# A new order of work inside the groups of a fused retention and feed-forward kernel

## The chip, the cores and the metric

The kernel runs on one core of a Trainium2 chip. A core has TensorE (PE in the profile; its weight loads are PEld), VectorE (DVE), ScalarE (ACT), GpSimd (POOL) and SyncE (SP, which here issues transfers). The time is device time in microseconds of one execution; a time of a version is the median of several runs. A profile is one execution recorded instruction by instruction.

## The reference

Two layers, one behind the other. The first is retention, linear attention with a decay for each of 8 heads; the second is a feed-forward pair of matrices with a leaky ReLU.

```python
def _attn_ref(q, k, v):                # 8 x 8 heads x 576 x 64
    scores = scale * np.matmul(q, k.transpose(0, 1, 3, 2))
    gamma = 1.0 - 2.0 ** (-5.0 - np.arange(H))
    Dmat = np.where(rel >= 0, gamma[:, None, None] ** rel[None], 0.0)   # rel = i - j
    return np.matmul(scores * Dmat[None], v)

def _moe_ref(x, w_in, w_out):          # x: 4608 tokens x 512, d_ff 2048
    h = x @ w_in
    g = np.maximum(0.01 * h, h)
    return g @ w_out
```

## The kernel before

The 4608 tokens are cut into 9 groups of 512 (`g` = 0 to 8) and 36 units of 128 (`u`, four to a group). A unit of retention is loaded (q, k, v), cast to 16 bits with its decay (`kc` on ScalarE, `qc` and `vc` on GpSimd), transposed by a transfer, and multiplied: scores and the state of two chunks of 64, then the outputs. While TensorE does the feed-forward part of group g, it does the retention of units that belong to the next group.

Retention of one unit, as steps of a group (`n` = 5 to 8, `u` = 4g + n):

```python
def mm():                        # "sc": scores of u, then outputs of the unit before
    if u < NU:
        scores(u)                # lines L225, L234; PSUM tile sc, one buffer
    outputs(u - 1)               # lines L316 (masked scores), L327 (state); PSUM tile ot
ops = {"sc": mm, "own": lambda: own(u - 1), "add": lambda: add(u - 1)}
ops["s0"] = lambda: state(u, 0)              # VectorE, L278 to L286
ops["s1a"] = lambda: state(u, 1, (0,))
ops["s1"] = lambda: state(u, 1, (1,))
ops["stc"] = lambda: state_cast(u, pool_copy)      # GpSimd, L298 and L301
if n < 7:
    ops["mc"] = lambda: masks_aside(u, 0)          # ScalarE copies the scores, L244
    ops["msk"] = lambda: masks_aside(u, 1)         # GpSimd masks them, L246
else:
    ops["msk"] = lambda: masks(u)                  # VectorE masks them, L255
# w = u + 2: the unit whose casts run in this step
ops["kc"] ... cast_k(w)   ops["qc"] ... cast_q(w, nc.gpsimd)   ops["vc"] ... cast_v(w, nc.gpsimd)
# when k and q are cast: transpose_dma(w), then load(u + 4)
```

The first product of the feed-forward part has 16 blocks of 128 columns of `w_in`. Four blocks at a time (a set: A = 0, 1, 8, 9; B = 2, 3, 10, 11; C = 4, 5, 12, 13) are done with seven products in place of eight, in the manner of Strassen and Winograd; this needs sums of the weights (`w_sum`, made once: `sum_w_in(f, n, engine)`, f = 0, 2, 4 for A, B, C), sums of x for each group (`x0` to `x3` on GpSimd, `sum_x`, L469), and sums of the products on VectorE. Blocks 6, 7, 14, 15 are done plainly, with four matmuls of 512 columns (L401).

```python
ops = {   # one set; a product is four matmuls of 256 columns, L498
    "p1": product("p1", ws(0, 0), xs(0, 0), True),   "k": keep(),               # ScalarE copy
    "p1'": product("p1", ws(0, 1), xs(1, 0), False), "g00": give(0, 0, "p1"),   # ScalarE, leaky
    "p6": product("p6", w(1), t(1), True),           "u": into(k, p6, k),       # VectorE, L487
    "p5": product("p5", w(0), t(0), True),           "v": fresh_sum("v", p5, k),
    "p7": product("p7", w(2), t(2), True),           "h4": into(v, p7, v),
    "p5'": product("p5", w(3), xs(1, 1), False),     "h5": fresh_sum("h", p5, k),
    "g11": give(1, 1, "v"),
    "p7'": product("p7", ws(1, 1), t(3), False),     "h4'": into(k, p7, k),
    "g01": give(0, 1, "h"),                          "g10": give(1, 0, "k"),
}
```

The second product (`w_out`) is done as one such set over the whole group: seven products of 16 matmuls of 256 columns (L636). Its sums of g are the mix sums of VectorE, in halves: `m00`, `m01`, `m10`, ... `m31` (L618, both inputs in SBUF). `m3` is written over a part of `gt` that P1 has read, and is an input of P5'; `m2` likewise for P7; P5 needs `m0`, P6 needs `m1`. `K` and `o00` are ScalarE copies, `U`, `V`, `o11`, `o01`, `o10` VectorE sums.

The order in which each engine gets its work is the order of this text; engines run their own queues in order and wait for each other only where data or buffers ask for it:

```python
GROUP = """
    p1A kA sc5 p6A qc5 s05 kc5 s1a5 p1'A mc5 p5A uA s15 blk15 own5 vA vc5 g00A add5 p7A
    msk5 stc5 l15 p1B h4A p5'A h5A kB sc6 kc6 p7'A p1'B p6B mc6 own6 s06 h4'A g00B blk7
    ...
    vc6 s17 qc7 l6 vc7 h4C stc7 kc7 h5C g11C add7 P1 g01C g10B m00 p7'C sc8 m01 own8 P5
    h4'C qc8 m10 m11 P6 K g10C m20 vc8 add8 m21 P7 kc8 U s08 V s1a8 m30 P1' x0 x1 m31 P5'
    s18 o11 x2 stc8 o00 msk8 P7' o01 o10 x3
"""
```

PSUM[...]: the tiles `sc` and `ot` take two each, and the four banks called `acc` go round among all products and blocks. The casts have four buffers, the loads five.

Groups 0 and 1 have an order of their own. Around the second product of groups 0 and 1:

```python
def burst(u, out=True):     # scores(u), outputs(u-1), VectorE's mask and state, GpSimd's state_cast
def ahead(u, between=None): # cast_k, cast_q (GpSimd), between(), cast_v (GpSimd), transpose
at = {
    ...
    12: lambda: [sum_w_in(0, n, nc.vector) for n in range(4)]
    + [nc.vector.tensor_copy(out=mask16, in_=mask_sb)],
    9: lambda: early(9, 12),                      # burst(9), ahead(12), load(15)
    13: lambda: [sum_w_in(2, n, nc.gpsimd) for n in range(4)],
}
... # second product of group 0 in 16 parts, with at[n] behind part n
burst(10)
ops = second_ops(1, {})
run("P1 K m30 m31")
early(11, 13)                                     # burst(11), ahead(13), load(16)
for n in range(4):
    sum_w_in(4, n, nc.gpsimd)
run("P1' o00 P6 U P5 V")
burst(12)
sum_x(2, (0, 1))
ahead(14, lambda: sum_x(2, (2, 3)))
load(17)
run("P7 o11 P5' o01 P7' o10")
```

Groups 2 to 7 follow `GROUP`, group 8 follows a list `LAST` without retention.

Of the kernel before, what the change touches and what calls it, by code (L numbers as in the profile page):

```python
# [18 lines left out]
def kernel(  # L19
# [9 lines left out]
    nc = tc.nc  # L29
    B, H, S, D = q.shape  # L30
# [53 lines left out]
    def behind(dma, *others):  # L84
        for o in others:
            tc.add_manual_dep(
                dma.ins,
                o.ins.name,
                mybir.DependencyInfo(
                    mybir.DependencyClass.Sync, mybir.DependencyReason.DATA  # L90
                ),
                reason="order of loads",
            )
# [6 lines left out]
    mask_sb = cs[:, NTAB : NTAB + CH]  # L100
# [9 lines left out]
    mask16 = idle[:, 0:CH]  # L110
# [10 lines left out]
    def load(u, eng=None, after=None, xs=(1, 0, 2)):  # L121
        for x in xs:
            t = ld_pool.tile([P, H, D], FP, name=f"t32_{x}")
            t32[u, x] = t
            c = 2 * u
            same = c % CB + 1 < CB
            e = eng[x] if isinstance(eng, dict) else eng or nc.sync
            engs = e if isinstance(e, tuple) else (e,)
            n = H // len(engs)
            for j, rows in ((0, P),) if same else ((0, CH), (1, CH)):  # L130
                b, w = (c + j) // CB, (c + j) % CB
                for i, e in enumerate(engs):
                    hs = slice(n * i, n * i + n)
                    d = e.dma_start(
                        out=t[CH * j : CH * j + rows, hs],
                        in_=(q, k, v)[x][b, hs, CH * w : CH * w + rows, :].rearrange(
                            "h t d -> t h d"
                        ),
                    )
                    if after is not None and (x in after or not isinstance(after, dict)):  # L140
                        behind(d, *(after[x] if isinstance(after, dict) else after))
                        after = None
                    last_load[u, x] = d
# [33 lines left out]
    def cast_k(u):  # L177
        nc.scalar.copy(out=qk_of(u)[:, 1], in_=t32[u, 1])

    def cast_q(u, eng):  # L180
        eng.tensor_tensor(out=qk_of(u)[:, 0], in0=t32[u, 0], in1=decay(u, 0), op=MUL)  # L181
# [71 lines left out]
    def masks(u):  # L253
        s16s[u] = b_pool.tile([P, 2, NP, CH], F16, name="s16")
        nc.vector.tensor_tensor(  # L255
            out=s16s[u],
            in0=sc_tiles[u][:, :, 0],
            in1=mask_sb.unsqueeze(1).unsqueeze(1).to_broadcast([P, 2, NP, CH]),
            op=MUL,
        )  # L260
# [34 lines left out]
    def state_cast(u, copy, js=(0, 1)):  # L295
        js = [j for j in js if live(u, j)]
        if len(js) == 2:
            copy(out=st16[u], in_=s32s[u])  # L298
        else:
            for j in js:  # L300
                copy(out=st16[u][:, j], in_=s32s[u][:, j])  # L301
# [79 lines left out]
    def own(u):  # L381
        owns[u] = b_pool.tile([P, NP, 2, CH], FP, name="own")
        nc.scalar.copy(  # L383
            out=owns[u], in_=ot_tiles[u][:, :, 0:NP].rearrange("q j c t -> q c j t")
        )
# [13 lines left out]
    def h_mm(hps, n, g, f, ts):  # L399
        for c in range(NP):  # L400
            nc.tensor.matmul(  # L401
                out=hps[:, n, :],
                lhsT=w_in16[:, c, f * P : (f + 1) * P],
                rhs=xT[g][:, c, ts],
                start=(c == 0),
                stop=(c == NP - 1),
            )

    def g_tile(g):
        if g not in g_t:  # L410
            g_t[g] = g_pool.tile([P, NF, TOK], F16, name="gt")
        return g_t[g]

    def leaky(out, in_):
        nc.scalar.activation(out=out, in_=in_, func=mybir.ActivationFunctionType.Lrelu)  # L415
# [23 lines left out]
    def w_sub(f, i, j):  # L439
        c0 = (f + i * HF) * P  # L440
        return w_in16[:, 2 * j : 2 * j + 2, c0 : c0 + 2 * P]

    def x_sub(g, j, k):
        return xT[g][:, 2 * j : 2 * j + 2, k * HT : (k + 1) * HT]

    def sum_w_in(f, n, eng):
        t = w_sum[:, f // 2]
        a, b, op = (
            (w_sub(f, 1, 0), w_sub(f, 1, 1), ADD),
            (t[:, 0], w_sub(f, 0, 0), SUB),  # L450
            (w_sub(f, 0, 0), w_sub(f, 1, 0), SUB),
            (w_sub(f, 0, 1), t[:, 1], SUB),
        )[n]
        eng.tensor_tensor(out=t[:, n], in0=a, in1=b, op=op)  # L454
# [3 lines left out]
    def sum_x(g, ns=range(4)):  # L458
        if g not in x_sums:
            x_sums[g] = s_pool.tile([P, 4, NP // 2, HT], F16, name="x_sum")  # L460
        t = x_sums[g]
        for n in ns:
            a, b = (
                (x_sub(g, 0, 1), x_sub(g, 0, 0)),
                (x_sub(g, 1, 1), t[:, 0]),
                (x_sub(g, 1, 1), x_sub(g, 0, 1)),
                (x_sub(g, 1, 0), t[:, 1]),
            )[n]
            nc.gpsimd.tensor_tensor(out=t[:, n], in0=a, in1=b, op=SUB)  # L469
# [10 lines left out]
    def bank(home, shape=(P, 2, HT)):  # L480
        pool, name = {
            None: (acc_pool, "acc"), "sc": (sc_pool, "sc"), "ot": (ot_pool, "ot")
        }[home]
        return pool.tile(list(shape), FP, name=name)
# [66 lines left out]
    def block_ops(g, f, homes):  # L551
        t = {}

        def mm():
            t["h"] = bank(homes.get(f"Bk{f}"), (P, 1, TOK))
            h_mm(t["h"], 0, g, f, slice(0, TOK))

        return {f"blk{f}": mm, f"l{f}": lambda: leaky(g_tile(g)[:, f : f + 1, :], t["h"])}
# [278 lines left out]
    def burst(u, out=True):  # L837

        scores(u)
        if out:  # L840
            outputs(u - 1)
        masks(u)
        state(u, 0)
        state(u, 1)
        state_cast(u, pool_copy)
        if out:
            own(u - 1)
            add(u - 1)

    def ahead(u, between=None):  # L850

        if u < NU:
            cast_k(u)
            cast_q(u, nc.gpsimd)
        if between is not None:
            between()
        if u < NU:
            cast_v(u, nc.gpsimd)
            transpose_dma(u)

    def step_ops(g, n):
# [39 lines left out]


    GROUP = """
        p1A kA sc5 p6A qc5 s05 kc5 s1a5 p1'A mc5 p5A uA s15 blk15 own5 vA vc5 g00A add5 p7A
        msk5 stc5 l15 p1B h4A p5'A h5A kB sc6 kc6 p7'A p1'B p6B mc6 own6 s06 h4'A g00B blk7
        msk6 s1a6 qc6 p5B uB p1C s16 vB g01A l7 p6C add6 g10A p7B kC h4B g11A p5'B stc6 p1'C
        g00C sc7 p7'B h5B uC s07 blk14 own7 msk7 p5C blk6 h4'B vC s1a7 p7C g11B p5'C g01B l14
        vc6 s17 qc7 l6 vc7 h4C stc7 kc7 h5C g11C add7 P1 g01C g10B m00 p7'C sc8 m01 own8 P5
        h4'C qc8 m10 m11 P6 K g10C m20 vc8 add8 m21 P7 kc8 U s08 V s1a8 m30 P1' x0 x1 m31 P5'
        s18 o11 x2 stc8 o00 msk8 P7' o01 o10 x3  # L910
    """
    LAST = """
        p1A blk6 p6A kA l6 uA p5A vA p7A p1'A p6B g00A p1B p5'A h4A kB h5A p6C p7'A uB p1'B
# [89 lines left out]
    def early(u, n):  # L1003
        burst(u)
        ahead(n)
        load(n + 3)
# [4 lines left out]
        3: lambda: mixes(1, 1),  # L1011
        4: lambda: (burst(8, False), ahead(11), load(13), load(14)),
        7: lambda: mixes(1, 2),
        12: lambda: [sum_w_in(0, n, nc.vector) for n in range(4)]
        + [nc.vector.tensor_copy(out=mask16, in_=mask_sb)],
        9: lambda: early(9, 12),
        13: lambda: [sum_w_in(2, n, nc.gpsimd) for n in range(4)],
    }
    for n in range(16):
        if n:  # L1020
            wide(n // 4, n % 4)
        if n in at:
            at[n]()
    burst(10)
    ops = second_ops(1, {})
    run = lambda names: [ops[n]() for n in names.split()]
    run("P1 K m30 m31")
    early(11, 13)
    for n in range(4):
        sum_w_in(4, n, nc.gpsimd)  # L1030
    run("P1' o00 P6 U P5 V")
    burst(12)
    sum_x(2, (0, 1))
    ahead(14, lambda: sum_x(2, (2, 3)))
    load(17)
    run("P7 o11 P5' o01 P7' o10")

    for g in range(2, NG):
        last = g == NG - 1
        homes = LAST_HOMES if last else {}  # L1040
        ops = second_ops(g, homes, last)
        for s, f in SETS.items():
            ops.update(set_ops(g, f, s, homes))
        for f in BLOCKS:
            ops.update(block_ops(g, f, homes))
        if not last:
            for n in range(5, 9):
                ops.update(step_ops(g, n))
            for n in range(4):
                ops[f"x{n}"] = lambda n=n: sum_x(g + 1, (n,))  # L1050
        for name in (LAST if last else GROUP).split():
            if name in ops:
                ops[name]()

# [29 lines left out]
```

## Time and profile before

| | |
|---|---|
| time, median of 3 runs | 292.82 us (292.59 to 293.51) |
| span of the profiled run | 292.1 us |
| mean granted clock of TensorE | 0.984 |
| HBM read, written | 36.81 MB, 9.44 MB |

The page of the profile starts with the busy time of each engine and its share of the span, then cuts the span into 40 equal slices of 7.3 us, in which each digit is a busy share in tenths:

```profile
PE   7899999997995999999999999999999999999993
DVE  2973888999763699889988997999799989977962
ACT  4767777432333671598059706870786078405900
POOL 8968847468799435774667466737573861160000
```

A busy TensorE is not a TensorE at its peak: the records overlap, and their ends are modelled. For its pace the starts of consecutive records are compared. The timeline lists instructions in order with the idle time before each and the engine whose signal ended it. "L618" is a line of the kernel; where a helper writes many tiles, all have its line, so the names of output and inputs tell them apart. The groups show in the slices as a period of about four digits from the 12th on.

### The profile page before, as it was taken

How to read it: one execution, taken by the hardware profiler on the slowest of the kernel's cores; microseconds unless marked ns; L12 is line 12 of the kernel's file. 1: busy time of each engine (PE TensorE's matmuls, PEld its weight loads, DVE VectorE, ACT ScalarE, POOL GpSimd, SP SyncE). 2: the span in 40 equal slices, each digit the busy share in tenths (PEclk: the TensorE clock that was granted, in tenths of full speed). 3: DMA queues.
4: the chain of work that ended last, by engine and by line, in shares of the span. 5: the costliest groups of instructions: out<-in, count | busy, mean ns of one | idle time of the engine just before them, and what ended most of it. 6: DMA issues, size and time to landing. Idle time of an engine off the chain costs nothing.

```text
span 292.1 us, 10069 instructions
## 1 busy us (share of the span) xinstructions
PE 276.1 (95%) x4317; PEld 214.3 (73%) x4317; DVE 240.5 (82%) x391; ACT 158.1 (54%) x291; POOL 170.1 (58%) x181
## 2 busy tenths in 40 slices
PE   7899999997995999999999999999999999999993
PEld 2578888545884677778777778788878787888782
DVE  2973888999763699889988997999799989977962
ACT  4767777432333671598059706870786078405900
POOL 8968847468799435774667466737573861160000
PEclk9999999999997799999999999999999999999998
DMA  8999999978999939888977788968988350002012
GB/s 223 292 223 219 289 209 328 209 162 198 251 215 274 186 73 217 165 191 181 189 211 175 172 173 191 200 143 195 201 196 182 42 183 3 0 36 109 2 38 108
DMA packets 123101, 50.05 MB, mean 171 GB/s; under 512 B 112048, under 2 KB 116784, under 8 KB 123056
## 3 DMA queue, kind: packets, MB, share of 16 engines
q1 hardware_dynamic: 116032, 37.23, 57.6%
q0 software_dynamic: 6736, 12.06, 17.2%
q8 instruction: 34, 0.56, 0.8%
q10 hardware_dynamic: 288, 0.11, 0.1%
q14 instruction: 11, 0.09, 0.1%
HBM read 36.81 MB, written 9.44 MB: 158 GB/s over the span
## 4 chain that ended last, share of the span: by engine, by line
PE 51%; DVE 33%; issue 6%; POOL 5%; ACT 2%; DMA 1%; DVEq 0%; POOLq 0%
PE acc L498 18%; PE acc L401 13%; PE acc L636 9%; DVE gt L618 7%; DVE mix L618 6%; DVE w_mix L599 4%; DVE k L487 3%; DVE xT L388 3%; DVE v L487 3%; PE sc L225 2%; POOL x_sum L469 2%; POOL w_sum L454 2%; DVE w_sum L454 2%; DVE h L487 1%; PE acc L708 1%
## 5 line engine op out<-in xcount | busy, mean ns | idle before, releaser
L636 PEld LDWEIGHTS <-gt 128*128 128x128 f16 x640 | 61.7, 98 | 11.7 <-DVE gt L618 4.1
L401 PE MATMUL acc<-xT,w_in 128*128 128x256 f16 (+2 forms) x376 | 58.6, 300 | 0.3 <-issue 0.3
L415 ACT ACTIVATE gt<-acc 128x512 f16<-128x512 f32 x77 | 45.8, 599 | 19.8 <-PE acc L401 14.6
L636 PE MATMUL acc<-w_out,gt 128*128 128x256 f16 x384 | 45.8, 273 | 2.4 <-DVE gt L618 2.3
L401 PEld LDWEIGHTS <-w_in 128*128 128x128 f16 x384 | 35.5, 98 | 11.4 <-issue 1.3
L498 PEld LDWEIGHTS <-w_sum 128*128 128x128 f16 x336 | 32.9, 99 | 10.7 <-issue 1.1
L487 DVE TENSOR_TENSOR k<-acc,k 128x512 f32<-128x512 f32 x48 | 32.6, 684 | 8.1 <-PE acc L498 6.1
L498 PE MATMUL acc<-x_sum,w_sum 128*128 128x256 f16 x244 | 36.3, 278 | 0.0
L469 POOL TENSOR_TENSOR x_sum<-xT 128x512 f16<-128x512 f16 x14 | 20.8, 1484 | 26.1 <-DVE xT L388 26.1
L185 POOL TENSOR_TENSOR v<-t,cs 128x512 f16<-128x512 f32 x28 | 30.8, 1101 | 0.5 <-DMA t<-in_v_dram 0.5
L181 POOL TENSOR_TENSOR qk<-t,cs 128x512 f16<-128x512 f32 x28 | 29.8, 1064 | 1.8 <-DMA t<-in_q_dram 1.7
L636 PE MATMUL acc<-w_mix,mix 128*128 128x256 f16 x256 | 29.8, 273 | 0.4 <-DVE mix L618 0.2
L636 PE MATMUL acc<-w_mix,gt 128*128 128x256 f16 x240 | 28.8, 272 | 0.0
L383 ACT COPY own<-ot 128x512 f32<-128x512 f32 x33 | 19.5, 590 | 16.6 <-PE ot L327 15.8
L521 ACT COPY k<-acc 128x512 f32<-128x512 f32 x19 | 11.1, 586 | 30.7 <-PE acc L498 30.5
L636 PEld LDWEIGHTS <-mix 128*128 128x128 f16 x256 | 24.1, 98 | 4.5 <-DVE mix L618 1.4
L498 PEld LDWEIGHTS <-w_in 128*128 128x128 f16 x252 | 24.1, 100 | 3.9 <-issue 0.2
L298 POOL CAST st<-s 128x512 f16<-128x512 f32 x21 | 12.8, 610 | 22.1 <-DVE s L284 18.2
L388 DVE TENSOR_TENSOR xT<-ot,own 128x512 f16<-128x512 f32 x33 | 22.5, 682 | 3.4 <-ACT own L383 3.4
L661 ACT COPY osb<-acc 128x512 f32<-128x512 f32 x8 | 4.7, 586 | 37.0 <-PE acc L636 37.0
L498 PE MATMUL acc<-xT,w_in 128*128 128x256 f16 x152 | 23.4, 277 | 0.0
L487 DVE TENSOR_TENSOR v<-acc,k 128x512 f32<-128x512 f32 x29 | 19.9, 686 | 4.1 <-PE acc L498 2.0
(95 smaller groups left out, 515.5 us busy)
## 6 DMA issues: line engine op xcount, KB each, us to landing
out_dram<-osb SPq DMA_DIRECT2D x17, 512.0 KB, 3.1
t<-in_k_dram SPq DMA_DIRECT2D x24, 256.0 KB, 3.7
t<-in_q_dram SPq DMA_DIRECT2D x23, 256.0 KB, 4.3
t<-in_v_dram SPq DMA_DIRECT2D x22, 256.0 KB, 4.4
t<-in_v_dram POOLq DMA_DIRECT2D x10, 256.0 KB, 5.9
t<-in_q_dram POOLq DMA_DIRECT2D x9, 256.0 KB, 5.6
t<-in_k_dram POOLq DMA_DIRECT2D x8, 256.0 KB, 7.5
w_in<-in_moe_w_in_dram POOLq DMA_DIRECT2D x8, 256.0 KB, 6.7
```

What stands on the lines that cost most here:

```text
L181: eng.tensor_tensor(out=qk_of(u)[:, 0], in0=t32[u, 0], in1=decay(u, 0), op=MUL)
L185: eng.tensor_tensor(out=v16[u], in0=t32[u, 2], in1=decay(u, 1), op=MUL)
L298: copy(out=st16[u], in_=s32s[u])
L383: nc.scalar.copy(out=owns[u], in_=ot_tiles[u][:, :, 0:NP].rearrange("q j c t -> q c j t"))
L388: nc.vector.tensor_tensor(out=x_of(u).rearrange("q (c g) t -> q c g t", g=2), in0=ot_tiles[u][:, :, NP : 2 * NP].rearrange("q g (c j) t -> ...
L401: nc.tensor.matmul(out=hps[:, n, :], lhsT=w_in16[:, c, f * P : (f + 1) * P], rhs=xT[g][:, c, ts], start=(c == 0), stop=(c == NP - 1),)
L415: nc.scalar.activation(out=out, in_=in_, func=mybir.ActivationFunctionType.Lrelu)
L469: nc.gpsimd.tensor_tensor(out=t[:, n], in0=a, in1=b, op=SUB)
L487: nc.vector.tensor_tensor(out=out, in0=a, in1=b, op=ADD)
L498: nc.tensor.matmul(out=r[name][:, n, :], lhsT=lhs()[:, c, n * P : (n + 1) * P], rhs=rhs()[:, c, :], start=fresh and n == 0 and c == 0, sto ...
L618: nc.vector.tensor_tensor(out=z[:, fs], in0=a[:, fs], in1=b[:, fs], op=op)
L636: nc.tensor.matmul(out=r[name][tb][:, 0, :] if apart else r[name][0][:, tb, :], lhsT=lhs()[:, f, tb * P : (tb + 1) * P], rhs=rhs[:, f, :], ...
```

## The change

Six edits:

1. The mask of 16 bits is cast by ScalarE and not by VectorE, and ahead of VectorE's weight sums.
2. The weight sums of set B (GpSimd) move from behind part 13 of group 0's second product to two places: two behind `burst(10)`, two behind the casts of units 13 and 14.
3. Unit 14 is cast with unit 13, ahead of P1', and no longer between the x sums of group 2. The loads of units 16 and 17 follow it.
4. Group 2 (the third) does set C as four plain blocks (4, 5, 12, 13), at the places of p1C, p6C, p5C and p7C.
5. So set C's weight sums are needed one group later; they move into group 2, still on GpSimd.
6. `GROUP` is a new order. Products and their sums stand closer to each other, unit 5 to 8's steps stand later, unit 8's scores stand behind P1', the mix sums are spread, `vc6`, `vc7`, `vc8`, `qc8` and the x sums stand later.

The aim is to keep VectorE's sums of two SBUF inputs and GpSimd's work apart in time, and to have unit 14 and GpSimd's masks ready sooner.

```diff
     GROUP = """
-        p1A kA sc5 p6A qc5 s05 kc5 s1a5 p1'A mc5 p5A uA s15 blk15 own5 vA vc5 g00A add5 p7A
-        msk5 stc5 l15 p1B h4A p5'A h5A kB sc6 kc6 p7'A p1'B p6B mc6 own6 s06 h4'A g00B blk7
-        msk6 s1a6 qc6 p5B uB p1C s16 vB g01A l7 p6C add6 g10A p7B kC h4B g11A p5'B stc6 p1'C
-        g00C sc7 p7'B h5B uC s07 blk14 own7 msk7 p5C blk6 h4'B vC s1a7 p7C g11B p5'C g01B l14
-        vc6 s17 qc7 l6 vc7 h4C stc7 kc7 h5C g11C add7 P1 g01C g10B m00 p7'C sc8 m01 own8 P5
-        h4'C qc8 m10 m11 P6 K g10C m20 vc8 add8 m21 P7 kc8 U s08 V s1a8 m30 P1' x0 x1 m31 P5'
-        s18 o11 x2 stc8 o00 msk8 P7' o01 o10 x3
+        p1A blk15 p6A kA p1'A g00A l15 p5A sc5 uA p7A kc5 vA p1B p5'A p6B s05 h4A own5 s1a5 kB
+        h5A p7'A s15 mc5 qc5 h4'A p1'B g00B g01A uB blk7 msk5 stc5 vc5 p5B l7 add5 p1C p7B sc6
+        g10A kC vB h4B g11A kc6 p5'B p1'C p7'B s06 h5B s1a6 p6C qc6 mc6 p5C msk6 g00C own6 g11B
+        h4'B uC blk6 p7C blk14 s16 vC vc6 add6 stc6 g01B g10B l6 p5'C l14 h4C sc7 g11C h5C p7'C
+        m00 qc7 g01C s07 h4'C m01 m10 P1 s1a7 m11 kc7 P5 own7 m20 K s17 P6 g10C m30 P1' msk7
+        stc7 add7 sc8 U m21 V m31 own8 P7 vc7 s08 add8 P5' o11 o00 x0 o01 kc8 P7' s1a8 qc8 x1
+        s18 x2 stc8 o10 x3 msk8 vc8
     """
...
-        12: lambda: [sum_w_in(0, n, nc.vector) for n in range(4)]
-        + [nc.vector.tensor_copy(out=mask16, in_=mask_sb)],
+        12: lambda: [nc.scalar.copy(out=mask16, in_=mask_sb)]
+        + [sum_w_in(0, n, nc.vector) for n in range(4)],
         9: lambda: early(9, 12),
-        13: lambda: [sum_w_in(2, n, nc.gpsimd) for n in range(4)],
     }
...
     burst(10)
+    for n in range(2):
+        sum_w_in(2, n, nc.gpsimd)
     ops = second_ops(1, {})
     run("P1 K m30 m31")
-    early(11, 13)
-    for n in range(4):
-        sum_w_in(4, n, nc.gpsimd)
+    burst(11)
+    ahead(13)
+    ahead(14)
+    load(16)
+    load(17)
+    for n in range(2, 4):
+        sum_w_in(2, n, nc.gpsimd)
     run("P1' o00 P6 U P5 V")
     burst(12)
-    sum_x(2, (0, 1))
-    ahead(14, lambda: sum_x(2, (2, 3)))
-    load(17)
+    sum_x(2)
     run("P7 o11 P5' o01 P7' o10")
+    PLAIN = {
+        "p1C": "blk4", "kC": "l4", "p6C": "blk12", "uC": "l12", "p5C": "blk5", "vC": "l5",
+        "p7C": "blk13", "h4C": "l13", "stc6": "stc6 w40", "qc7": "qc7 w41 w42", "vc8": "vc8 w43",
+    }
+    third = " ".join(PLAIN.get(name, name) for name in GROUP.split())
...
+        if g == 2:
+            ops = {n: op for n, op in ops.items() if n[-1] != "C"}
+            for f in (4, 5, 12, 13):
+                ops.update(block_ops(g, f, homes))
+            for n in range(4):
+                ops[f"w4{n}"] = lambda n=n: sum_w_in(4, n, nc.gpsimd)
...
-        for name in (LAST if last else GROUP).split():
+        for name in (LAST if last else third if g == 2 else GROUP).split():
```

## The prediction

> **What bounds the kernel now.** I read the table of busy time first, then the slices with the granted clock, then TensorE's timeline around each place where the slices dip, and last the timelines of the engine that TensorE waited for there. (The group of tokens g = 2 is called the third group; its units are 12 to 15.)
>
> ```profile
> PE 276.1 (95%) x4317; PEld 214.3 (73%) x4317; DVE 240.5 (82%) x391; ACT 158.1 (54%) x291; POOL 170.1 (58%) x181
> PEclk9999999999997799999999999999999999999998
> ```
>
> TensorE is busy for 95% of the span, so rearranging can only win where it stands still or runs slowly. The clock row has two slices at 7, from about 88 to 102 us, and nothing like it elsewhere. The timeline of TensorE around them:
>
> ```profile
> 71.59 0.32 PE L225 MATMUL sc<-qkT 64*64 64x64 f16 x16 [1.92 <-DVE s L286]
> ...
> 89.15 0.32 PE L225 MATMUL sc<-qkT 64*64 64x64 f16 x16 [0.37 <-DMA qkT<-qk]
> 89.37 0.32 PE L234 MATMUL sc<-v,qk 64*64 64x64 f16 x16
> 92.47 0.43 PE L316 MATMUL ot<-s,v 64*64 64x64 f16 x16 [2.79 <-POOL s L246]
> ...
> 94.73 1.06 PE L498 MATMUL acc<-x_sum,w_sum 128*128 128x256 f16 x4
> 95.59 1.91 PE L401 MATMUL acc<-xT,w_in 128*128 128x512 f16 x4
> ```
>
> The columns are start, duration, engine, line, operation, output<-inputs, count, and in brackets the idle time and who ended it. Three things are to be seen: a wait of 1.92 us for VectorE's state of unit 10, waits of 0.37 and 2.79 us for unit 14's transposed copy and for GpSimd's masked scores of unit 13, and after the last one matmuls at half speed (four of 256 columns in 0.86 us from start to start, against 0.44 elsewhere). The view by windows gives the size of that:
>
> ```profile
> 89.00:92.50 3.50, 0.56 (x36) 0.45 (x37) 0.94 (x2) 1.07 (x2) 3.50 (x5) 0.87 1.03 240
> 92.50:98.80 6.30, 6.30 (x57) 4.06 (x57) 2.12 (x4) 2.82 (x5) 4.25 (x6) 0.53 1.25 260
> ```
>
> The last three numbers are granted clock, DMA share and GB/s; the five before are busy times of TensorE, its weight loads, VectorE, ScalarE and GpSimd. GpSimd is busy for all of the first stretch while TensorE does 0.56 us of work; in the second the clock is 0.53. So 6.3 x (1 - 0.53) = 2.96 us go to the clock. GpSimd's own timeline there runs without a break from 74.99 to 93.84, with four weight sums (77.57 to 82.19), four x sums and six casts ahead of the mask at 91.28.
>
> In the steady groups the only wait named is this, once a group:
>
> ```profile
> 174.06 1.05 PE L636 MATMUL acc<-w_out,gt 128*128 128x256 f16 x8 [0.47 <-DVE gt L618]
> ```
>
> It is the second half of product P5', waiting for VectorE's m31. The same point comes at 116.51, 145.09, 174.06, 202.62, 231.50 and 259.51 us, so a group takes (259.51 - 116.51) / 5 = 28.6 us.
>
> **What the skill says.** SBUF — State Buffer, section "Who interferes with whom": a VectorE instruction with two SBUF inputs contends with a GpSimd instruction that reads SBUF. The mix sums have two SBUF inputs, and the trace agrees: one form has instances of 678 and of 1639 ns.
>
> ```profile
> L618 DVE TENSOR_TENSOR mix<-gt x16: 678/684/1534, 56.7 to 275.7; 128x1024 f16<-128x1024 f16 x16
> L618 DVE TENSOR_TENSOR gt<-gt,mix x16: 678/1347/1639, 72.0 to 279.3; 128x1024 f16<-128x1024 f16 x16
> ```
>
> The long ones (163.91 to 166.04, 171.56 to 174.0) lie over GpSimd's casts and x sums (163.90, 171.85). TensorE: Matmul & The Clock Gate, section "What's actually happening": the clock falls to half after an idle window of about 3.4 us and comes back after as long a busy one. The trace shows the fall at an idle stretch of about 3 us and a recovery some 6 us later, so the page is right in kind; the 6 us is the number I use.
>
> **The change part by part.**
>
> *VectorE in the second group.* Before, VectorE makes four weight sums from 64.04 to 68.45 and casts the mask (1.14 us) before it may take unit 10; TensorE's 1.92 us follow from that. The cast goes to ScalarE, which is idle much of that time (1.19 us before 69.71), and GpSimd's own four weight sums (66.92 to 71.7), which overlapped VectorE's, move behind unit 10's state. VectorE's sums took 0.83, 1.15, 1.26 and 1.37; the last two, freed of GpSimd, should be nearer 0.8 each. That is 1.06 + about 1.0 = 2.1 us earlier against 1.92 to be hidden. I count 1.7.
>
> *GpSimd ahead of the third group.* Set C's four weight sums leave (4 x 1.12 = 4.5 us) because the third group no longer uses set C; unit 14's casts come before the x sums. Walked by hand with the durations of the trace: unit 10's state by 70.1, two sums to 72.4, unit 11's state 73, casts of 13 and 14 to 77.1, two sums 79.4, unit 12's state 80, x sums to 84.6, the cast of unit 15 to 85.7, mask of 13 at about 86.8. The third group starts on TensorE near 82 (83.86 less the 1.7); in the new order outputs(13) stand 8.6 us into it, at about 90.8. The mask is ready 4 us before and unit 14's transpose likewise. The waits of 0.37 + 2.79 go: 3.1. Without a stop that long the clock should not fall: 2.9.
>
> *Four plain blocks.* A set is 28 matmuls of 256 columns, 28 x 0.109 = 3.05 us (0.436 per product); four plain blocks are 16 of 512 columns, 16 x 0.215 = 3.44. It costs 0.4 once on TensorE and takes five sums of 0.60 off VectorE. The moved weight sums then lie in GpSimd's idle time of that group.
>
> *The new order in the groups.* TensorE's ideal group: 21 first products x 0.436 = 9.16, four blocks x 0.86 = 3.44, four attention units x 0.74 = 2.96, seven second products x 1.745 = 12.2, together 27.8 us. So 28.6 holds 0.8 us of waits. From h5C to the end of m31 the old order takes about 10 us of VectorE, 2 of them contention (6.9 us for eight mix sums that take 0.6 each alone). The new order puts the x sums after m31, the late casts beside sums that read PSUM, and unit 8's scores ahead of P7, which gives m20, m21 and m31 0.74 us more. By hand: P1 at 14.84 us into the group, P7's second half needs m21 at 23.45 and m21 is done at about 23.3; P5' needs m31 at 25.2, and it is done at 24.5 to 25. Both just fit, with nothing to spare, so I take 28.15 and not 27.8: 0.45 x 5 = 2.25. In the third group itself about 1.0 us of small waits (34.9 - 27.8 - 3.16 - 2.96) becomes 0.4: 0.6.
>
> Sum: 1.7 + 3.1 + 2.9 - 0.4 + 0.6 + 2.25 = 10.15, which makes 292.8 - 10.15 = 282.7. The start to 60 us, and the last group from 262 on, keep their code. I add 0.8 for waits that a hand walk doesn't see: 283.5.
>
> **Rivals.** (1) VectorE becomes the bound of the groups. It carries about 26.4 us of work in 28.9 (the windows view gives 26.53 for 118.8 to 147.7); the new order makes its queue, which is in order, follow TensorE more closely, so one late u or h4 holds a PSUM bank and then a product. Against it: less contention takes up to 2 us off. If it comes, groups stay at 28.6 or go to 29: 286 to 288. (2) The stop moves instead of going: unit 15 or 16 is cast later, and GpSimd's first mask of the third group waits behind the x sums. The slack by my walk is 4 us, so this needs a late load; loads at 92 to 99 us run at a DMA share above 1, so it isn't absurd. A stop of 3 us would bring the half clock too and leave 289. (3) The clock falls anyway, from several shorter waits: +3, 286.5. (4) VectorE's weight sums don't shorten, and 0.9 of the 1.92 stays: 284.4.
>
> **Range and chances.** The removed stop and its clock (6.0 us) are the firm part: the trace shows both, and 4 us of slack take the mask's place. The 2.25 in the groups is the soft part, anywhere from -2 to +4. So the middle is 283.5, the range 280.0 to 289.0. 2% faster is below 287.0; only rivals 1 and 2 together or a new stop miss it: 0.80. Within 2% 0.15, slower 0.05.
>
> **What would show it.** Right: the clock row has no 7 near slice 13; GpSimd's mask L246 no longer ends a long wait of TensorE; the wait on L286 is gone or below 0.4; the wait on gt L618 ahead of P5' is under 0.2; gt<-gt,mix has a median near 0.7 us; the third group takes about 28.6 us from its first product to the next group's, the others 28.15. Wrong: a stop over 2 us anywhere between 60 and 120 us, or groups of 28.6 and more with TensorE waiting for VectorE's u, h4 or k sums.

## The result and the profile after

The changed kernel takes 284.38 us (283.55 to 286.22) against 293.16: a ratio of 0.971, with a 95% interval of 0.966 to 0.976. Measured again beside other versions it took 283.73 (0.967, 0.964 to 0.971). The prediction was 283.5.

From the page of the changed kernel, the busy times and the granted clock (the share of its full clock that TensorE was given, in tenths):

```profile
PE 271.8 (96%) x4305; PEld 212.8 (75%) x4305; DVE 227.8 (80%) x385; ACT 153.9 (54%) x291; POOL 165.8 (58%) x181
PEclk9999999999999999999999999999999999999998
```

The two slices at 7 are gone, and VectorE has lost 12.7 us of work (240.5 to 227.8). To see where the span went, I cut it at the first product p1A of each group, as the timelines of TensorE show it, and at the first mix sum of group 1 on VectorE:

| stage | before | changed | changed, second profile |
|---|---|---|---|
| start to the first mix sum | 56.72 | 59.45 | 56.87 |
| from there to the third group | 27.14 | 26.59 | 26.62 |
| third group | 35.32 | 28.66 | 28.66 |
| groups 3 to 7, each | 28.59 | 27.96 | 27.98 |
| last group to the end | 29.96 | 29.90 | 29.94 |
| span | 292.1 | 284.4 | 282.0 |

The first stage has the same code in both kernels. The 2.7 us by which the first profile of the changed kernel is later stand beside loads that landed later (VectorE waits 5.4 us for a load of q there against 3.9, and TensorE waits 1.0 us for one of w_in where it didn't before), and the second profile shows that they don't belong to the change. Against that second profile the span falls by 10.1 us: 6.7 in the third group, 3.05 in the five groups behind it, 0.5 ahead of it. The last group is untouched. These are single profiles: that of before has a low clock (0.984), and between the medians of the timed runs lie 8.8 us, or 9.45 the second time.

TensorE's timeline of the changed kernel, with the scores of unit 12, the point where the third group stopped before (scores of 14 and outputs of 13), and the second product of a steady group:

```profile
80.15 0.32 PE L225 MATMUL sc<-qkT 64*64 64x64 f16 x16 [1.41 <-DMA qkT<-qk]
...
94.71 0.32 PE L225 MATMUL sc<-qkT 64*64 64x64 f16 x16
94.86 0.30 PE L234 MATMUL sc<-v,qk 64*64 64x64 f16 x16
94.99 0.30 PE L316 MATMUL ot<-s,v 64*64 64x64 f16 x16
...
165.37 1.92 PE L636 MATMUL acc<-w_mix,gt 128*128 128x256 f16 x16
167.12 1.91 PE L636 MATMUL acc<-w_out,gt 128*128 128x256 f16 x16
```

There is no bracket at 94.99 any more: nothing is waited for. Nor at 167.12, which is P5' with all 16 matmuls in one piece; before, it was cut in two by the wait for m31. But 80.15 shows a wait that was not there before. The rows of the mix sums say why P5' no longer waits:

```profile
L618 DVE TENSOR_TENSOR mix<-gt x16: 675/683/1712, 59.4 to 268.0; 128x1024 f16<-128x1024 f16 x16
L618 DVE TENSOR_TENSOR gt<-gt,mix x16: 676/682/1637, 72.8 to 271.7; 128x1024 f16<-128x1024 f16 x16
```

The second row is m30 and m31; its median went from 1347 to 682 ns.

### The profile page after: what moved, and what is told of

Same layout as the page of the kernel before. It is cut to its first block, busy times and chain, and to the rows that moved or that the text cites. A ratio compares the mean times of both kernels' runs of the same rounds, so it can differ in the third digit from the quotient of the medians.

```text
span 284.4 us, 10057 instructions
## 1 busy us (share of the span) xinstructions
PE 271.8 (96%) x4305; PEld 212.8 (75%) x4305; DVE 227.8 (80%) x385; ACT 153.9 (54%) x291; POOL 165.8 (58%) x181
## 4 chain that ended last, share of the span: by engine, by line
PE 68%; DMA 15%; POOL 6%; DVE 5%; issue 5%; ACT 1%; POOLq 0%; DVEq 0%; ACTq 0%
PE acc L636 30%; PE acc L498 19%; PE acc L401 9%; POOL t L134 4%; DMA w_out<-in_moe_w_out_dram 3%; DMA w_in<-in_moe_w_in_dram 3%; DMA t<-in_v_dram 3%; DMA t<-in_k_dram 3%; PE sc L225 2%; PE acc L574 2%; DMA qkT<-qk 2%; PE ot L327 1%; POOL w_in L152 1%; PE sc L234 1%; PE ot L316 1%
## 5 line engine op out<-in xcount | busy, mean ns | idle before, releaser
L401 PE MATMUL acc<-xT,w_in 128*128 128x256 f16 (+2 forms) x392 | 61.1, 301 | 1.3 <-DMA w_in<-in_moe_w_in_dram 1.0
L498 PEld LDWEIGHTS <-w_sum 128*128 128x128 f16 x320 | 30.3, 98 | 9.7 <-issue 0.3
L487 DVE TENSOR_TENSOR k<-acc,k 128x512 f32<-128x512 f32 x46 | 30.6, 684 | 4.7 <-PE acc L498 3.9
L498 PE MATMUL acc<-x_sum,w_sum 128*128 128x256 f16 x232 | 33.9, 273 | 0.1
L469 POOL TENSOR_TENSOR x_sum<-xT 128x512 f16<-128x512 f16 x14 | 16.1, 1153 | 24.4 <-DVE xT L388 24.4
L185 POOL TENSOR_TENSOR v<-t,cs 128x512 f16<-128x512 f32 x28 | 29.3, 1048 | 0.0
L298 POOL CAST st<-s 128x512 f16<-128x512 f32 x21 | 14.1, 671 | 21.1 <-DVE s L284 13.3
L487 DVE TENSOR_TENSOR osb<-acc,k 128x512 f32<-128x512 f32 (+1 forms) x16 | 10.8, 675 | 15.3 <-PE acc L636 15.3
L178 ACT CAST qk<-t 128x512 f16<-128x512 f32 x36 | 22.3, 620 | 1.4 <-DMA t<-in_k_dram 1.4
L246 POOL TENSOR_TENSOR s<-s,idle 128x512 f16<-128x512 f16 x12 | 13.9, 1158 | 15.5 <-ACT s L244 15.5
```

The source lines that it names most:

```text
L185: eng.tensor_tensor(out=v16[u], in0=t32[u, 2], in1=decay(u, 1), op=MUL)
L401: nc.tensor.matmul(out=hps[:, n, :], lhsT=w_in16[:, c, f * P : (f + 1) * P], rhs=xT[g][:, c, ts], start=(c == 0), stop=(c == NP - 1),)
L487: nc.vector.tensor_tensor(out=out, in0=a, in1=b, op=ADD)
L498: nc.tensor.matmul(out=r[name][:, n, :], lhsT=lhs()[:, c, n * P : (n + 1) * P], rhs=rhs()[:, c, :], start=fresh and n == 0 and c == 0, sto ...
```

## The experiments

Theory A was the prediction's: GpSimd's shorter queue (edits 2, 3 and 5) removes the stop in the third group, and the new order (edit 6) only shortens the groups. Theory B, which I formed as its rival when I read the new trace: the order alone removes the stop, because it puts the outputs of unit 13 later in the group. Theory C concerns the new wait at 80.15. A ratio compares runs at normal speed, taken together with runs of the kernel before (medians 293.2 to 293.3 us), and can differ by some tenths of a per cent from the quotient of the medians.

**The old order with the rest of the change.** The `GROUP` of before in the changed kernel.

```diff
-        p1A blk15 p6A kA p1'A g00A l15 p5A sc5 ...      # the new GROUP
+        p1A kA sc5 p6A qc5 s05 kc5 s1a5 p1'A ...        # the old one, whole
```

> The changed kernel with the old order of GROUP put back: edits 1 to 5 without edit 6. Theory A (as predicted: GpSimd's shorter queue removes the stop in the third group, the order only its 0.7 us per group): the stop of 2.8 us on the mask and the half clock are gone, groups 3 to 7 stay at 28.6 us with the 0.47 us wait for m31, time about 284.4 + 5 x 0.65 = 287.6. Theory B (the stop went because the new order puts outputs(13) 8.6 us into the third group and not 5.3): TensorE waits again for the mask of unit 13, by 1 to 3 us, perhaps with the half clock, time 289 to 293.

Measured: 290.42 us, ratio 0.991 (0.987 to 0.994). The third group takes 31.21 us, the groups behind it 28.71. TensorE's timeline:

```profile
89.05 0.32 PE L316 MATMUL ot<-s,v 64*64 64x64 f16 x16 [1.16 <-POOL s L246]
...
95.81 0.32 PE L225 MATMUL sc<-qkT 64*64 64x64 f16 x16 [0.99 <-DMA qkT<-qk]
```

The first is the wait for the mask: it shrank from 2.79 to 1.16 us, and did not go. A second one came, for unit 15's transposed copy. Edits 1 to 5 alone are worth a third of the gain.

**The new order alone.**

```diff
-        p1A kA sc5 p6A qc5 s05 kc5 s1a5 p1'A ...        # the old GROUP
+        p1A blk15 p6A kA p1'A g00A l15 p5A sc5 ...      # the new one, in the kernel before
```

> The kernel before with only the new GROUP: edit 6 without 1 to 5. Theory A: the stop for GpSimd's mask in the third group stays (2 us or more) with the half clock behind it, groups take 28.05 us; time about 293.2 - 3.5 = 289.7. Theory B: the new order alone takes the stop away, since outputs(13) now stand 3.3 us later; the wait of 1.92 us on unit 10's state stays; time about 293.2 - 3.5 - 6 = 283.7 to 285.

Measured: 284.73 us, ratio 0.973 (0.969 to 0.977). The third group takes 27.97 us, the others 27.93, and TensorE has one named wait behind 60 us:

```profile
71.91 0.32 PE L225 MATMUL sc<-qkT 64*64 64x64 f16 x16 [1.91 <-DVE s L286]
```

Theory B holds: edit 6 by itself gives 8.5 of some 9 us, with GpSimd's work ahead of the third group as it was. GpSimd's timeline has the mask of unit 13:

```profile
92.37 1.16 POOL L246 TENSOR_TENSOR s<-s,idle 128x512 f16<-128x512 f16 x1 [1.54 <-ACT s L244]
```

GpSimd stands idle ahead of it even here, so its queue, set C's sums included, no longer decides. The new order also puts one cast of unit 15 (`vc5`, 1.04 us) behind the mask and not ahead of it; that would have fitted into the 1.54 us. The outputs start at 94.30, 0.8 us after the mask's end.

**The stop filled.** Twelve matmuls of constant data ahead of the real outputs of unit 13.

```diff
         ot = ot_pool.tile([P, 2, 2 * NP, CH], FP, name="ot")
+        for _ in range(12 if u == 13 else 0):
+            nc.tensor.matmul(out=ot[:, 0]..., lhsT=idle[:, P : 2 * P], rhs=idle, start=True, stop=True)
```

> The kernel before with 12 extra matmuls of 512 columns on constant data (about 2.6 us) put between scores(14) and outputs(13), into a tile that the real outputs overwrite; the wait stays, but TensorE works through it. If the half clock comes from the stop: no slice at half clock, time 293.2 - 2.9 = 290.3. If the clock falls for another reason: the 0.53 of 92.5 to 98.8 us stays and the time is 293 or more.

Measured: 293.08 us, ratio 1.000 (0.998 to 1.002). Timeline of TensorE:

```profile
91.75 2.76 PE L311 MATMUL ot<-idle 128*128 128x512 f16 x12
94.45 0.32 PE L322 MATMUL ot<-s,v 64*64 64x64 f16 x16
...
101.11 0.32 PE L225 MATMUL sc<-qkT 64*64 64x64 f16 x16 [1.31 <-DMA qkT<-qk]
```

And by windows (busy times of TensorE, weight loads, VectorE, ScalarE, GpSimd; then clock, DMA share, GB/s):

```profile
72.00:75.00 3.00, 2.56 (x72) 1.98 (x73) 3.00 (x6) 1.10 (x2) 1.11 (x2) 0.65 1.13 286
75.00:78.00 3.00, 3.00 (x23) 2.46 (x22) 1.22 (x3) 0.59 (x1) 2.21 (x3) 0.78 1.12 156
93.00:96.00 3.00, 3.00 (x51) 1.89 (x49) 0.53 (x1) 0.68 (x2) 2.69 (x4) 1.00 1.14 367
```

Behind the filled stop the clock is whole (93 to 96), where the profile of before has 0.53. But in this profile it fell behind the other stop, that of 1.9 us near 70, where the profile of before has 1.00; so one profile alone doesn't show what the filling did. The timed runs do, for each has a span and a mean clock. Span x (1 - clock), the time lost to the clock, averages 1.2 us over the 20 runs of this version and 2.2 over the 27 of the kernel before taken with them: the stop costs clock, but about 1 us on average and not 2.9. The spans hardly follow (291.3 us against 291.5). At full speed TensorE ran into unit 15's transposed copy, 1.31 us too early, so a half clock here stretches work that would have waited anyway. Over 50 runs of the kernel before, the loss averages 2.4 us, and a straight line through them gives 0.36 us of span for each microsecond so lost; the two sets of runs taken alone give 0.51 and 0.11, so that only "well below 1" is shown. Over the four first runs of the changed kernel the loss is 0.8.

**No plain blocks in the third group.** Edits 4 and 5 undone.

```diff
     for n in range(2, 4):
         sum_w_in(2, n, nc.gpsimd)
+    for n in range(4):
+        sum_w_in(4, n, nc.gpsimd)
...
-        if g == 2:
+        if False:
-        for name in (LAST if last else third if g == 2 else GROUP).split():
+        for name in (LAST if last else GROUP).split():
```

> The changed kernel with set C as a set in the third group too, and its four weight sums on GpSimd ahead of the x sums (edits 4 and 5 undone). Theory A (the weight sums in GpSimd's queue are what the plain blocks were worth): x1 and with it p6A of the third group come 4.5 us later, about 3.5 us of stop on TensorE, perhaps the half clock: 287 to 291. Rival (the plain blocks only shift work, GpSimd has slack): 284.4 - 0.4 = 284.

Measured: 288.9 us (286.21 to 290.71), ratio 0.989 (0.983 to 0.995).

```profile
88.27 0.60 PE L498 MATMUL acc<-x_sum,w_sum 128*128 128x256 f16 x4 [3.51 <-POOL x_sum L469]
```

This is p6A, 3.5 us late, as theory A had it for this run. Yet the version with the new order alone has set C's weight sums on GpSimd ahead of the third group too and doesn't wait there. The difference is in edits 2 and 3, which put the last two of set B's weight sums (2.3 us of GpSimd's time) and unit 14's two casts (2.0 us) ahead of the x sums. The plain blocks take out what these edits put in.

**The front of before with the rest of the change.** Edits 2 and 3 undone.

```diff
         9: lambda: early(9, 12),
+        13: lambda: [sum_w_in(2, n, nc.gpsimd) for n in range(4)],
...
-    burst(11); ahead(13); ahead(14); load(16); load(17); ... sum_w_in(2, n, nc.gpsimd)
+    early(11, 13)
...
-    sum_x(2)
+    sum_x(2, (0, 1))
+    ahead(14, lambda: sum_x(2, (2, 3)))
+    load(17)
```

> The changed kernel with edits 2 and 3 undone: the weight sums of set B early on GpSimd and unit 14 cast between the x sums, as before; the new order, the plain blocks and ScalarE's mask cast stay. If edits 2 and 3 are what readies unit 14 and the mask: a stop over 1 us comes back in the third group, 285.5 or more. If they only trade the wait of VectorE (1.9 us at unit 10) for that of unit 12's transpose (1.4 us), the time is 283.5 to 284.7, as the changed kernel, with a wait near 0.8 us at unit 10.

Measured: 285.81 us, ratio 0.973 (0.969 to 0.977), beside 283.73 for the changed kernel.

```profile
70.07 0.32 PE L225 MATMUL sc<-qkT 64*64 64x64 f16 x16 [0.81 <-DVE s L286]
72.38 0.26 PE L327 MATMUL ot<-qkT,st 64*64 64x64 f16 x8 [1.42 <-POOL st L298]
```

The 0.81 is as expected; no stop came back in the third group (28.66 us). But a second wait appears right behind, for a state that GpSimd casts only when its weight sums are through, and in this profile the clock fell after the two. From the first mix sum to the third group it takes 29.18 us and not 26.62. That is what edits 2 and 3 are worth with the rest of the change: about 2 us, ahead of the third group and not in it. Neither outcome written down beforehand came as it was put.

**The mask on VectorE again.** Edit 1 undone.

```diff
-        12: lambda: [nc.scalar.copy(out=mask16, in_=mask_sb)]
-        + [sum_w_in(0, n, nc.vector) for n in range(4)],
+        12: lambda: [sum_w_in(0, n, nc.vector) for n in range(4)]
+        + [nc.vector.tensor_copy(out=mask16, in_=mask_sb)],
```

> The changed kernel with the mask cast on VectorE again, behind the weight sums (edit 1 undone). Unit 10's state comes 1.1 us later, so scores(11) wait about 1 us. Theory C (unit 12's transposed copy, which TensorE waits for 1.41 us in the changed kernel, is set by SyncE's queue and hides 1 us of it): the wait at unit 12 shrinks by as much and the time stays 284.4. Rival: both waits stand, 285.4.

Measured: 283.34 us, ratio 0.965 (0.959 to 0.970), no slower than the changed kernel; but not for the reason expected. scores(11) don't wait at all, and unit 12's wait is still 1.27 us. VectorE's timeline and a line of GpSimd's, in that version and then before:

```profile
67.06 0.41 DVE L454 TENSOR_TENSOR w_sum<-w_in,w_sum 128x512 f16<-128x512 f16 x1
67.40 0.18 DVE L1015 CAST idle<-cs 128x64 f16<-128x64 f32 x1
...
69.87 0.61 POOL L298 CAST st<-s 128x512 f16<-128x512 f32 x1 [3.02 <-DVE s L286]
```

```profile
67.16 1.37 DVE L454 TENSOR_TENSOR w_sum<-w_in,w_sum 128x512 f16<-128x512 f16 x1
68.45 1.14 DVE L1015 CAST idle<-cs 128x64 f16<-128x64 f32 x1
...
68.32 1.22 POOL L454 TENSOR_TENSOR w_sum<-w_sum,w_in 128x512 f16<-128x512 f16 x1
```

The same cast takes 0.18 us and not 1.14, the same sum 0.41 and not 1.37, once GpSimd has no weight sums of its own at that time (it is idle for the 3.02 us up to 69.87). Edit 2 had already freed VectorE; edit 1 does nothing more. Without edit 2 it does: in the version with the front of before the wait was 0.81 us and not 1.92.

**Unit 14's loads behind unit 12's transpose.** Theory C.

```diff
-        4: lambda: (burst(8, False), ahead(11), load(13), load(14)),
+        4: lambda: (burst(8, False), ahead(11), load(13)),
-        9: lambda: early(9, 12),
+        9: lambda: (burst(9), ahead(12), load(14), load(15)),
```

SyncE's queue in the changed kernel, with the transpose of unit 12 as its last line:

```profile
71.36 0.58 SPq L134 DMA_DIRECT2D t<-in_k_dram  x1
72.03 0.53 SPq L134 DMA_DIRECT2D t<-in_q_dram  x1
72.65 1.66 SPq L134 DMA_DIRECT2D t<-in_v_dram  x1
74.40 0.80 SPq L564 DMA_DIRECT2D out_dram<-osb  x1
75.37 1.91 SPq L189 DMA_TRANSPOSE qkT<-qk  x1
```

> The changed kernel with the loads of unit 14 issued behind unit 12's transpose and not ahead of it. Theory C (SyncE issues one after the other, 0.5 to 1 us each, and the transpose of unit 12 stands behind three loads too many): the wait of 1.41 us on unit 12 goes, time 284.4 - 1.4 = 283.0, if the casts of unit 14 do not wait for their loads. Rival (the transfer itself is slow, or the wait moves to unit 13 or 14): 284.4.

Measured: 283.45 us, ratio 0.965 (0.960 to 0.971). The wait for unit 12 is gone, and this has come:

```profile
84.39 0.60 PE L498 MATMUL acc<-x_sum,w_sum 128*128 128x256 f16 x4 [1.39 <-POOL x_sum L469]
```

**Both queues.** The same, and on GpSimd the first two x sums ahead of set B's last two weight sums.

```diff
-    for n in range(2, 4):
-        sum_w_in(2, n, nc.gpsimd)
     run("P1' o00 P6 U P5 V")
     burst(12)
-    sum_x(2)
+    sum_x(2, (0, 1))
+    sum_w_in(2, 2, nc.gpsimd); sum_x(2, (2,)); sum_w_in(2, 3, nc.gpsimd); sum_x(2, (3,))
```

> The changed kernel with the loads of unit 14 behind unit 12's transpose and, on GpSimd, the first two x sums ahead of the last two weight sums of set B. Putting the loads back alone only moved the wait of 1.4 us from SyncE's queue to GpSimd's x sum. If these two queues are all that stands there, both waits go and the time is the changed kernel's less 1.2 us, near 282.5. Rival: a third queue stands behind (add of unit 11 on VectorE, or the weight sums needed by p7A), and the time stays within 0.4 us of the changed kernel.

Measured: 283.33 us, ratio 0.965 (0.962 to 0.968). The two waits are gone; the third group is 0.9 us longer instead:

```profile
97.92 0.32 PE L225 MATMUL sc<-qkT 64*64 64x64 f16 x16 [1.23 <-DMA qkT<-qk]
```

This is unit 15's transposed copy, SyncE's queue again: it had been late in the old order too (0.99 and 1.31 us above). Theory C is half right. The wait for unit 12 is SyncE's order, but with it gone, 1.2 to 1.4 us of waiting turned up at the next place each time. That SyncE's and GpSimd's queues from 60 to 98 us together hold TensorE to this pace is the reading that fits; no run lightens both. The gain over the changed kernel, 0.4 us, lies inside the intervals.

**add8 late in the old order.** The x sums away from m30 and m31.

```diff
-        h4'C qc8 m10 m11 P6 K g10C m20 vc8 add8 m21 P7 kc8 U s08 V s1a8 m30 P1' x0 x1 m31 P5'
+        h4'C qc8 m10 m11 P6 K g10C m20 vc8 m21 P7 kc8 U s08 V s1a8 m30 P1' m31 add8 x0 x1 P5'
```

> The kernel before with add8, x0 and x1 behind m31, so that GpSimd's x sums no longer run beside m30 and m31. If sums with two SBUF inputs are slowed by GpSimd's reads, m30 and m31 fall from 1.2 us each to 0.6, the 0.47 us wait of P5' goes in each of the groups 2 to 6, time 293.2 - 5 x 0.45 = 290.9. Rival (the length of VectorE's queue, not the contention, sets m31): m31 just as late, 293.2; or the x sums, now later, hold p6A of the next group: slower.

Measured: 292.58 us, ratio 0.997 (0.995 to 0.999). VectorE's m30 and m31, and then a wait of TensorE in the next group:

```profile
170.57 1.28 DVE L618 TENSOR_TENSOR gt<-gt,mix 128x1024 f16<-128x1024 f16 x2
```

```profile
152.42 0.26 PE L327 MATMUL ot<-qkT,st 64*64 64x64 f16 x8 [0.17 <-POOL st L298]
```

m30 and m31 take 1.28 us together and not 2.44 (before, at 171.56), and the wait of P5' is gone from every group. The groups still take 28.8 us: the x sums, now later, delay GpSimd's state cast behind them, and small waits stand in several places, some 0.3 us in a group by name; where the rest goes is not shown. Contention made m31 late, as predicted; taking it away in the old order brings the groups nothing.

**GpSimd busy beside the mix sums in the new order.** Four extra sums of spare data in each of the groups 3 to 7; they add work and leave none out.

```diff
-        m00 qc7 g01C s07 h4'C m01 m10 P1
+        m00 qc7 d0 d1 d2 d3 g01C s07 h4'C m01 m10 P1
+        # dn: nc.gpsimd.tensor_tensor(out=spare, in0=idle, in1=idle, op=ADD)
```

> The changed kernel with four extra sums on GpSimd (f16, 128 x 512, on spare data) behind qc7 in the groups 3 to 7, where GpSimd idled 4.9 us beside m00 to m20. If contention is what cost the old order its group time: the five mix sums there take about 0.5 us longer each, m21 and m31 come 2 to 2.5 us later, TensorE waits 0.3 to 0.9 us in each group, time 284.4 + 2 to 4. Rival (the new order has slack enough by itself): the mix sums are longer but TensorE waits less than 0.1 us, time as the changed kernel.

Measured: 288.7 us, ratio 0.983 (0.976 to 0.989); 29.01 us a group. The mix sums alone, by windows of one group, in the changed kernel and then in this version (VectorE's busy time, clock, DMA share, GB/s):

```profile
142.76:170.80 28.04, 5.22 (x8) 1.00 0.85 188
```

```profile
141.33:170.59 29.26, 7.30 (x8) 1.00 0.81 183
```

VectorE's eight mix sums go from 5.2 to 7.3 us (the old order had 7.1), and each group is 1.05 us longer. TensorE's timeline names the mix sums as the cause:

```profile
161.72 1.05 PE L637 MATMUL acc<-w_mix,mix 128*128 128x256 f16 x8 [0.40 <-DVE mix L619]
```

So keeping the two engines apart is a condition of the new order's 28.0 us: with the contention back, it is no better than the old one.

**One move of the new order in the old one.** sc6 behind p7', p1', p6 and the block 7.

```diff
-        ... h5A kB sc6 kc6 p7'A p1'B p6B mc6 own6 s06 h4'A g00B blk7 msk6
+        ... h5A kB kc6 p7'A p1'B p6B h4'A g00B blk7 sc6 mc6 own6 s06 msk6
```

> The kernel before with one thing of the new order only: sc6 (scores of unit 14 and outputs of unit 13 in the third group) behind p7', p1', p6 and the block 7, 2.2 us of TensorE's work later. Theory B (the place of the outputs decides over the stop): the wait for the mask falls from 2.8 to about 0.6 us, and the time by 1 to 2 us (unit 15's transposed copy stands next), 291.2 to 292.2, groups stay 28.6. Rival: the mask comes as much later as the outputs do, wait and time as before.

Measured: 301.32 us, ratio 1.024 (1.020 to 1.029). The first of these lines is the third group's outputs of unit 13, the last a steady group:

```profile
92.88 0.32 PE L316 MATMUL ot<-s,v 64*64 64x64 f16 x16 [0.50 <-POOL s L246]
...
98.70 0.32 PE L225 MATMUL sc<-qkT 64*64 64x64 f16 x16 [1.85 <-DMA qkT<-qk]
...
189.74 1.05 PE L498 MATMUL acc<-x_sum,w_sum 128*128 128x256 f16 x8 [1.42 <-DVE k L487]
```

The wait for the mask fell to 0.50 us, where 0.6 was expected: the place of the outputs does decide. But the move applies to all groups, and they went to 30.26 us, with products that wait for VectorE's k sums. The time I expected was wrong by 9 us: this one move without the others costs more than the stop.

**The changed kernel again,** beside the front of before, both queues and the one move.

> The changed kernel unaltered, beside the next three on the same chip: 283.5 to 284.7, with the wait of 1.3 to 1.4 us for unit 12's transposed copy.

Measured: 283.73 us, with a wait of 1.45 us for unit 12.

## Why the prediction was right, and where it wasn't

*The total* (283.5 against 284.38 and 283.73) holds. That the sum of its terms (10.15 us) meets the 10.1 between two profiles is luck: the second group fell 1.2 us short of its term, the third group and those behind it together came out 1.3 above theirs, and the profile of before had a poor clock.

*The stop in the third group.* It went, as predicted (3.1), and the third group takes 28.66 us where 28.6 was predicted. The cause given was wrong: "The mask is ready 4 us before". In the changed kernel GpSimd is idle for 3.07 us ahead of it, waiting for ScalarE's copy of the scores:

```profile
92.63 1.16 POOL L246 TENSOR_TENSOR s<-s,idle 128x512 f16<-128x512 f16 x1 [3.07 <-ACT s L244]
```

The mask ends at 93.79 and the outputs start at 94.99, so 1.2 us ahead; the slack comes from the later place of the step, whose scores start 8.7 us into the group and 5.3 before. The walk had that place (8.6), and credited the gain to GpSimd's queue all the same; it overlooked that the new order also takes ScalarE's copy of the scores, which the mask needs, later. The new order alone removes the stop; the shorter queue alone leaves 1.16 us.

*The clock.* "Without a stop that long the clock should not fall: 2.9" was right in kind and too large in general. The profile of before happened to have the worse case (a clock of 0.984; the 50 runs average 0.992), and time lost by the clock counts in the span for well below its length. The version with add8 late, whose order is the old one until near the end of the third group, gives a second look: its profile has the half clock behind the wait for unit 10's state (0.50 from 73 to 76 us), then waits 1.54 us for the mask and not 2.79, and its third group takes 31.95 us and not 35.32. So a part of the 6.7 us is that one profile's.

*VectorE in the second group.* Counted 1.7; the stage gave 0.5. The 1.92 us did go, but a wait of 1.4 us for unit 12's transposed copy took their place, which none of the rivals named: the walk followed the engines that compute, and not SyncE's queue, which issues three loads and a store ahead of it. Within the step, of the two sums that should shorten to about 0.8 us one stayed at 1.26, beside GpSimd's casts, and the other took 0.41; and of the cast's 1.06 us only 0.18 were its own.

*Four plain blocks.* Predicted +0.4, measured 28.66 - 27.97 = +0.7 against the third group of the new order alone. What they buy is GpSimd's time, and only because edits 2 and 3 spend it. The 0.6 of small waits in that group was counted from a length of 34.9 us; by the first products it was 35.32.

*The groups.* Predicted 28.15, measured 27.97: 3.05 us in place of 2.25. The walk was cautious on contention; with none, m31 is done 1.2 us before P5' starts (165.89 against 167.12) and not just in time. Rival 1, VectorE as the bound, didn't come: it has 24.4 us of work in 28.04.

*Rivals 2 and 3*, a stop that moves and a clock that falls anyway, didn't come in the changed kernel, but each came in one of its variants.

## What to carry to other kernels

When a wait ends on an engine's queue, ask both how to make that queue shorter and how to put the waiting work later; here the second did nearly everything. Edits that lean on each other mislead when undone singly: the plain blocks then look worth some 4 us, and edits 1 to 5 together bring 0.4 to 1.0 us on top of the order, with intervals that overlap. When a stop is removed, add up what the next engine can deliver there, the queue that issues transfers included: that bounds the gain. Work on GpSimd cost VectorE time here where sums of two SBUF inputs lay beside it, and so did one cast with a single input; with the mix sums moved away from it, they took 0.68 us each.

## What the runs showed of the hardware

A VectorE cast of 128 x 64 numbers took 0.18 us alone and 1.14 us beside GpSimd's sums, and one of its sums 0.41 alone against 1.37: here the neighbour cost more than the work. GpSimd loses too: its weight sums took up to 1.60 us beside mix sums and 1.15 alone. The section "What's actually happening" of TensorE: Matmul & The Clock Gate in the Trainium skill speaks of an idle window of about 3.4 us. These runs are looser. The same wait for the state of unit 10, 1.85 to 1.92 us long, was followed by a clock of 0.50 to 0.58 (73 to 76 us) in three profiles, the order alone, the filled stop and add8 late, and by none in two, before and the one move. A stop of 3.5 us was followed by none in the profile without plain blocks, whose mean clock is 1.000; its three other runs have 0.978 to 0.990. A free-running window, which the page also states, would fit that; no run here tests it.
